# A new hand-written order, and two loads moved ahead of another, in a one-core kernel of chunked attention and a cosine feed-forward layer

## The chip, the core and the metric

One core of a Trainium2 chip runs the whole program. It has five engines with queues of their own: TensorE (PE in the profile, its weight loads PEld), VectorE (DVE), ScalarE (ACT), GpSimd (POOL) and SyncE (SP), which issues nearly all loads and stores. The metric is device time in microseconds (us) of one execution; less is better. Fast comparisons use the median of several runs.

## The reference

```python
scores = scale * np.matmul(q_c, k_c.transpose(0, 1, 2, 4, 3))   # chunks of 64 positions, 8 x 8 heads
scores = scores - np.max(scores, axis=-1, keepdims=True)
attn = np.exp(scores)
attn = attn / (np.sum(attn, axis=-1, keepdims=True) + 1e-09)
out = np.matmul(attn, v_c)
...
x = np.ascontiguousarray(attn_out.transpose(0, 2, 1, 3)).reshape(B * S, H * D)   # 4608 x 512
h = x @ w_in            # 512 x 2048
g = h * np.cos(h)
return (g @ w_out).astype(np.float32)    # 2048 x 512
```

Attention has batch 8, 8 heads, 576 positions and head size 64, and looks only within chunks of 64 positions. Its rows are the 4608 tokens of the layer behind it.

## The kernel before

The tokens are cut into tiles of 512. For each tile the kernel loads queries and keys (`qt`, `kt`) and values (`vt`) of four pairs of heads, 256 KB each, and makes for each pair: the scores on TensorE; their largest value, the difference, the exponential, its sum and the quotient on VectorE, ScalarE and GpSimd; the transposes of the result on TensorE (`transposed`, L656) with a copy to `pts`; and the products with the values (`acc<-pts,vt`). The weighted values are split into a high and a rest part (`weighted`, L736 and L739), which are the tile's `x`. Then come `h<-x,w_in` and, after h * cos(h), `acc<-w_out,g`. Each product of 32-bit numbers is made of three matmuls on such parts (`x_hi`, `x_lo`). w_in and w_out lie in 16 blocks each, which arrive as 64-bit numbers, 512 KB a block, and are made into 32-bit parts by ScalarE (`half`, L434, and `w`, L432), VectorE (L427) and GpSimd or VectorE. For the later tiles, products are made from sums and differences of blocks of 256 rows, seven products in place of eight; their sums go out to memory (`sums`, `diffs`, `combo`) and come back by loads (`block_pair`, `g_load`, `w_load`).

All of this is cut into 3646 pieces. `piece` appends each to the list `work`, with its engine, the pieces it waits for and, for some, another engine that may do it. Nothing of it runs in the order of that list. RANK is a table written out by hand into the program: it gives each piece its place in one order over all engines, and each engine gets its pieces in that order. ELSEWHERE lists the pieces that run on their other engine (a copy by VectorE instead of ScalarE, a TENSOR_TENSOR by GpSimd instead of VectorE, or the reverse). So each engine's queue is fixed, and an instruction whose input isn't there holds back everything behind it.

Ahead of the pieces stand loads: FIRST_LOADS is a list of 24, issued one after the other by SyncE at the start (`load`, L348). `('qk', 1, 0)` is queries and keys of the second tile's first pair of heads, `('in', 0)` the first block of w_in, `('v', 0, 0)` the first values. For the first tile `load_qk` gives the keys to ScalarE's queue (L481); for the others both to SyncE's. The buffers of `qt` and `kt` are four each, so that the second tile's first pair takes the place of the first tile's first pair.

For the attention of the first tile the work of one head pair runs through several engines, and the order decides which of the pieces of four pairs goes first. The numbers of pieces named below are places in `work`.

Of the kernel before, what the change touches and what calls it, by code (L numbers as in the profile page):

```python
# [71 lines left out]
    ('qk', 0, 0), ('qk', 0, 1), ('qk', 0, 2), ('qk', 0, 3), ('in', 1), ('qk', 1, 0),  # L72
    ('in', 0), ('v', 0, 0), ('v', 0, 1), ('in', 2), ('v', 0, 2), ('in', 4),
# [19 lines left out]
    27, 24, 33, 39, 42, 45, 15, 59, 68, 71, 54, 58, 64, 77, 81, 83, 69, 87, 96, 110, 90, 80, 115, 121, 125, 120, 92,  # L93
    134, 144, 148, 130, 139, 143, 146, 149, 155, 142, 167, 170, 173, 161, 172, 177, 182, 186, 176, 174, 180, 188,
    190, 189, 185, 194, 197, 201, 195, 192, 204, 212, 216, 213, 205, 222, 225, 227, 219, 221, 232, 238, 241, 233,
    229, 236, 247, 252, 244, 262, 264, 268, 273, 258, 270, 272, 277, 281, 279, 271, 291, 295, 298, 283, 284, 288,
    306, 322, 308, 299, 312, 314, 317, 327, 313, 331, 339, 341, 330, 316, 335, 345, 347, 346, 354, 357, 360, 369,
    356, 348, 362, 370, 373, 371, 377, 388, 391, 393, 382, 365, 387, 396, 397, 400, 390, 404, 407, 409, 403, 394,
    406, 416, 420, 424, 413, 442, 444, 448, 426, 435, 438, 441, 452, 453, 449, 459, 464, 468, 458, 440, 462, 466,
    472, 0, 13, 1, 3, 4, 5, 2, 7, 8, 12, 6, 9, 11, 17, 10, 22, 28, 31, 18, 26, 36, 14, 16, 20, 23, 30, 35, 41, 50,  # L100
    19, 21, 25, 37, 46, 40, 47, 29, 34, 38, 49, 56, 43, 53, 44, 51, 60, 63, 74, 65, 70, 57, 61, 67, 75, 79, 73, 76,
    32, 48, 55, 66, 78, 84, 86, 89, 88, 94, 98, 102, 93, 101, 105, 108, 72, 91, 137, 156, 95, 104, 99, 159, 168,
    171, 111, 114, 109, 112, 117, 200, 147, 150, 128, 131, 181, 231, 178, 223, 245, 251, 256, 255, 259, 52, 62, 82,
    85, 100, 107, 116, 119, 124, 127, 97, 103, 106, 113, 118, 123, 126, 129, 132, 136, 122, 135, 140, 145, 153, 158,
    162, 141, 151, 138, 133, 154, 152, 163, 165, 175, 179, 184, 169, 157, 166, 160, 164, 187, 191, 202, 209, 218,
    220, 183, 198, 196, 203, 193, 199, 207, 210, 214, 217, 234, 215, 224, 206, 208, 211, 226, 230, 235, 243, 246,
    250, 228, 254, 239, 237, 242, 240, 248, 253, 261, 266, 269, 267, 276, 274, 294, 249, 257, 275, 280, 282, 293,
    305, 307, 278, 263, 292, 260, 265, 286, 290, 296, 300, 303, 309, 301, 287, 289, 297, 285, 304, 527, 302, 525,
    321, 532, 318, 530, 548, 311, 315, 319, 324, 326, 328, 310, 333, 323, 332, 336, 334, 337, 340, 343, 349, 350,
    344, 320, 325, 329, 353, 352, 359, 363, 366, 368, 372, 367, 358, 338, 351, 342, 375, 378, 380, 383, 385, 386,  # L110
    384, 364, 355, 395, 361, 398, 401, 405, 408, 422, 427, 402, 376, 374, 381, 379, 411, 414, 417, 425, 428, 432,
    410, 429, 433, 419, 423, 445, 455, 457, 469, 474, 480, 489, 492, 497, 500, 508, 512, 544, 562, 528, 547, 554,
    555, 557, 565, 566, 571, 576, 574, 596, 575, 578, 586, 593, 597, 603, 613, 620, 636, 640, 421, 399, 392, 389,
    415, 431, 436, 439, 443, 446, 454, 437, 434, 467, 470, 430, 447, 450, 456, 465, 485, 487, 451, 476, 460, 473,
    479, 461, 471, 475, 483, 491, 495, 481, 463, 478, 499, 498, 490, 493, 496, 504, 507, 514, 486, 505, 494, 509,
    502, 510, 513, 515, 516, 521, 524, 511, 545, 503, 517, 559, 518, 526, 529, 541, 561, 564, 523, 543, 546, 534,
    520, 535, 538, 542, 551, 553, 558, 550, 536, 573, 556, 540, 567, 584, 587, 591, 594, 598, 560, 595, 583, 580,
    589, 570, 581, 590, 602, 604, 612, 601, 569, 592, 577, 585, 608, 610, 622, 625, 629, 633, 616, 628, 609, 607,
    611, 634, 638, 621, 623, 617, 631, 619, 626, 627, 630, 635, 637, 641, 642, 632, 656, 624, 643, 650, 645, 654,
    658, 668, 676, 677, 647, 671, 652, 646, 667, 661, 663, 666, 679, 689, 692, 675, 686, 662, 664, 659, 685, 695,  # L120
    699, 701, 705, 714, 700, 696, 690, 694, 717, 710, 712, 715, 718, 729, 735, 708, 734, 725, 731, 722, 720, 728,
    733, 740, 744, 747, 737, 418, 412, 533, 552, 599, 588, 660, 519, 477, 482, 484, 488, 539, 501, 506, 522, 531,
    579, 537, 549, 563, 568, 606, 572, 582, 600, 605, 615, 614, 618, 639, 644, 670, 648, 649, 674, 688, 697, 698,
    702, 653, 719, 750, 703, 713, 730, 758, 651, 657, 673, 680, 687, 721, 691, 742, 678, 732, 669, 684, 682, 711,
    672, 681, 655, 665, 723, 727, 716, 724, 736, 739, 726, 753, 766, 767, 772, 799, 801, 790, 793, 822, 824, 811,
    817, 830, 872, 885, 928, 910, 902, 916, 931, 943, 980, 992, 1007, 1031, 1008, 1020, 1075, 1049, 1072, 1079,
    1091, 1087, 1095, 1103, 1114, 1122, 1120, 1152, 1159, 1197, 1179, 1201, 1215, 1211, 749, 738, 842, 754, 765,
    757, 741, 826, 761, 783, 819, 776, 785, 880, 821, 889, 893, 816, 864, 895, 683, 693, 709, 746, 756, 763, 704,
    707, 745, 751, 774, 786, 780, 792, 796, 807, 868, 871, 878, 743, 748, 752, 755, 760, 771, 759, 762, 764, 769,
    778, 813, 805, 886, 891, 894, 904, 927, 938, 706, 777, 768, 770, 787, 775, 773, 779, 794, 782, 781, 784, 812,  # L130
    789, 788, 791, 804, 795, 798, 802, 806, 803, 810, 809, 815, 797, 800, 808, 827, 832, 836, 841, 844, 814, 820,
    825, 829, 818, 823, 828, 833, 835, 838, 862, 845, 847, 858, 851, 853, 940, 876, 896, 874, 861, 865, 921, 945,
    899, 905, 870, 883, 930, 988, 948, 890, 866, 898, 831, 834, 839, 857, 907, 909, 854, 877, 879, 884, 914, 929,
    936, 962, 964, 968, 971, 976, 979, 837, 840, 843, 846, 849, 860, 848, 852, 855, 863, 901, 961, 944, 983, 999,
    1003, 1013, 1033, 1038, 850, 856, 859, 873, 867, 869, 875, 903, 881, 882, 888, 900, 887, 892, 906, 908, 911,
    915, 913, 919, 923, 918, 922, 924, 926, 934, 897, 912, 917, 925, 952, 957, 969, 974, 920, 950, 954, 967, 932,
    935, 939, 946, 949, 953, 1036, 990, 986, 993, 981, 1024, 1040, 1048, 1055, 1074, 985, 989, 1000, 1078, 1025,
    996, 991, 1006, 1012, 1016, 1086, 1043, 933, 937, 941, 942, 951, 955, 958, 960, 959, 987, 956, 963, 977, 966,
    965, 970, 973, 998, 972, 975, 984, 995, 978, 982, 1022, 1002, 1005, 1026, 1009, 1014, 1017, 1011, 1021, 1019,
    1023, 1052, 994, 997, 1004, 1010, 1037, 1047, 1051, 1062, 1015, 1018, 1029, 1050, 1027, 1030, 1034, 1041, 1054,  # L140
    1068, 1076, 1112, 1090, 1110, 1085, 1089, 1099, 1153, 1127, 1146, 1092, 1101, 1148, 1115, 1133, 1131, 1100,
    1116, 1160, 1156, 1150, 1164, 1028, 1032, 1042, 1044, 1046, 1053, 1056, 1057, 1058, 1060, 1065, 1064, 1063,
    1067, 1071, 1073, 1070, 1080, 1083, 1082, 1081, 1094, 1118, 1097, 1102, 1161, 1105, 1108, 1163, 1107, 1111,
    1119, 1123, 1128, 1098, 1104, 1109, 1113, 1125, 1132, 1135, 1140, 1121, 1126, 1138, 1147, 1129, 1142, 1145,
    1151, 1117, 1130, 1136, 1154, 1143, 1139, 1155, 1158, 1220, 1172, 1225, 1249, 1261, 1169, 1245, 1252, 1157,
    1162, 1236, 1229, 1178, 1176, 1167, 1168, 1231, 1250, 1181, 1244, 1248, 1234, 1256, 1258, 1059, 1066, 1061,
    1084, 947, 1039, 1069, 1077, 1141, 1174, 1173, 1185, 1088, 1134, 1144, 1149, 1182, 1192, 1170, 1093, 1177, 1186,
    1001, 1045, 1096, 1137, 1180, 1184, 1124, 1165, 1190, 1195, 1175, 1189, 1106, 1199, 1035, 1191, 1166, 1171,
    1183, 1188, 1200, 1187, 1194, 1193, 1218, 1196, 1203, 1209, 1204, 1208, 1207, 1198, 1202, 1205, 1214, 1217,
    1223, 1228, 1232, 1206, 1210, 1221, 1226, 1213, 1219, 1224, 1242, 1237, 1246, 1312, 1297, 1309, 1295, 1240,  # L150
    1243, 1255, 1259, 1238, 1272, 1265, 1270, 1274, 1375, 1314, 1356, 1286, 1280, 1285, 1283, 1290, 1264, 1300,
    1308, 1212, 1216, 1230, 1233, 1247, 1257, 1227, 1235, 1239, 1254, 1262, 1263, 1267, 1271, 1275, 1327, 1330,
# [2430 lines left out]
```

## Time and profile before

| | us |
|---|---|
| median of three runs | 773.69 |
| the three runs | 773.27, 773.69, 774.88 |
| profiled execution | 774.28 |
| its span, from the first to the last instruction | 772.3 |
| TensorE busy in the span | 756.1 |
| VectorE busy | 678.9 |
| ScalarE busy | 529.7 |
| GpSimd busy | 343.0 |

The profiled execution stands 0.59 us above the median; 1.98 us of it lie outside the span. Busy time of an engine is the time in which any of its instructions runs. Matmuls overlap a little, and the ends given for them are modelled, so the times from start to start say more than their durations. A wait is put down to what came last. In brackets a timeline shows the idle time before an instruction and what ended it.

### The profile page before, as it was taken

What the parts mean: (1) busy time and instruction counts of PE and PEld (TensorE: products, weight loads), DVE (VectorE), ACT (ScalarE), POOL (GpSimd) and SP (SyncE); (2) the same over time, 40 slices, a digit from 0 to 9 for tenths busy, and PEclk for the clock granted to TensorE, in tenths of its full rate; (3) what the DMA queues carried; (4) which work ended last, traced back from release to release, by engine and by line L of the source; (5) the groups of instructions that cost most, each with busy time, mean ns of one, the idle gap of its engine ahead of it and who ended that gap; (6) DMA issues with size and microseconds to landing.
All of it is one profiled execution on the core that took longest, in us unless ns stands there. A gap on an engine that the chain in (4) does not pass through costs nothing. (4 is left out here: it accounts for less than half of the span.)

```text
span 772.3 us, 18060 instructions
## 1 busy us (share of the span) xinstructions
PE 756.1 (98%) x6680; PEld 684.6 (89%) x6680; DVE 678.9 (88%) x1138; ACT 529.7 (69%) x1064; POOL 343.0 (44%) x329
## 2 busy tenths in 40 slices
PE   7999999999999999999989999999999999999998
PEld 6788888888999888888889998888899989989997
DVE  5998889988999998989979989989999889878975
ACT  5998787465885556878876649879686556567532
POOL 1521224745589325745732235547601236454233
PEclk9999999999999999999999999999999999999999
DMA  9995023199989857898899956898899557999982
GB/s 347 409 418 217 1 94 115 53 328 339 375 306 317 290 176 266 285 324 267 301 337 348 351 196 224 273 327 314 295 378 337 190 184 253 310 315 328 360 288 90
DMA packets 127000, 210.92 MB, mean 273 GB/s; under 512 B 11712, under 2 KB 67008, under 8 KB 126912
## 3 DMA queue, kind: packets, MB, share of 16 engines
q1 hardware_dynamic: 126336, 208.71, 78.4%
q8 instruction: 53, 0.87, 0.4%
q10 hardware_dynamic: 576, 1.05, 0.4%
q14 instruction: 35, 0.29, 0.1%
HBM read 148.90 MB, written 60.82 MB: 272 GB/s over the span
## 5 line engine op out<-in xcount | busy, mean ns | idle before, releaser
L352 PE MATMUL h<-x,w_in 128*128 128x512 f32 (+1 forms) x960 | 225.4, 365 | 0.4 <-DVE w_in L373 0.2
L352 PEld LDWEIGHTS h<-x,w_in 128*128 128x128 f32 x960 | 168.8, 190 | 22.1 <-DVE g L777 0.7
L352 PE MATMUL acc<-w_out,g_hi 128*128 128x512 f32 (+1 forms) x720 | 172.5, 329 | 0.0
L352 PEld LDWEIGHTS acc<-w_out,g_hi 128*128 128x128 f32 x720 | 124.0, 190 | 12.5
L352 PE MATMUL acc<-w_out,g_lo 128*128 128x512 f32 (+1 forms) x360 | 117.4, 326 | 0.0
L352 PE MATMUL h<-w_in,w_in 128*128 128x512 f32 (+1 forms) x384 | 98.6, 355 | 1.3 <-ACT h L1018 1.1
L373 POOL TENSOR_TENSOR w_in<-w_in,w_in 128x512 f32<-128x512 f32 (+2 forms) x41 | 48.8, 1195 | 60.0 <-ACT w_in L1031 22.2
L352 PEld LDWEIGHTS h<-w_in,w_in 128*128 128x128 f32 x384 | 65.5, 190 | 10.7 <-ACT h L1018 2.9
L352 PEld LDWEIGHTS acc<-w_out,g_lo 128*128 128x128 f32 x360 | 68.6, 190 | 4.7
L369 ACT CAST g_hi<-w_in 128x512 fp32r<-128x512 f32 x71 | 44.0, 623 | 34.7 <-PE acc L352 16.2
L1031 ACT ACTIVATE w_in<-w_in 128x512 f32<-128x512 f32 x96 | 57.8, 628 | 12.1 <-DVE w_in L1027 11.8
L373 POOL TENSOR_TENSOR g_lo<-w_in,g_hi 128x512 fp32r<-128x512 f32 x32 | 42.0, 1314 | 36.6 <-ACT g_hi L369 18.5
L373 DVE TENSOR_TENSOR g_lo<-w_in,g_hi 128x512 fp32r<-128x512 f32 x62 | 45.5, 738 | 5.8 <-ACT g_hi L369 3.5
L369 ACT CAST g_hi<-x 128x512 fp32r<-128x512 f32 x52 | 32.2, 623 | 22.7 <-PE acc L352 12.0
L373 POOL TENSOR_TENSOR g_lo<-x,g_hi 128x512 fp32r<-128x512 f32 x9 | 12.3, 1376 | 75.7 <-ACT g_hi L369 75.7
L1024 ACT ACTIVATE w_in<-w_in 128x512 int32<-128x512 f32 x56 | 34.2, 627 | 16.2 <-DVE w_in L1021 11.9
L352 PE MATMUL a<-w_in,w_in 128*128 128x512 f32 (+1 forms) x204 | 43.1, 350 | 0.9 <-ACT w_in L369 0.6
L352 PE MATMUL a<-x,w_in 128*128 128x512 f32 (+1 forms) x192 | 41.2, 353 | 0.0
L352 PE MATMUL acc<-w_in,g_hi 128*128 128x256 f32 x240 | 41.0, 275 | 0.0
L1027 DVE SCALAR_TENSOR_TENSOR w_in<-w_in,w_in 128x512 f32<-128x512 int32 x56 | 37.8, 698 | 3.4 <-ACT w_in L1024 2.8
L373 DVE TENSOR_TENSOR g_lo<-x,g_hi 128x512 fp32r<-128x512 f32 x47 | 35.4, 766 | 5.3 <-ACT g_hi L369 5.1
L352 PE MATMUL acc<-x,g_hi 128*128 128x256 f32 x232 | 39.6, 275 | 0.0
(318 smaller groups left out, 1942.4 us busy)
## 6 DMA issues: line engine op xcount, KB each, us to landing
w_in<-combo SPq DMA_DIRECT2D x84, 512.0 KB, 5.4
w_in<-sums SPq DMA_DIRECT2D x64, 256.0 KB, 5.1
combo<-w_in SPq DMA_DIRECT2D x56, 256.0 KB, 4.3
w_in<-combo SPq DMA_DIRECT2D x56, 256.0 KB, 5.4
x<-sums SPq DMA_DIRECT2D x48, 256.0 KB, 5.0
qt<-in_qT_dram SPq DMA_DIRECT2D x36, 256.0 KB, 5.4
w_in<-in_w_in_dram SPq DMA_DIRECT2D x16, 512.0 KB, 9.5
kt<-in_kT_dram SPq DMA_DIRECT2D x32, 256.0 KB, 5.4
```

The source lines that it names most:

```text
L352: kept(nc.tensor.matmul(*args, **kw))
L369: kept(nc.scalar.copy(out=out, in_=in_))
L373: kept(eng.tensor_tensor(out, a, b, op=op))
L1024: kept(nc.scalar.activation(g.bitcast(I32), h, AF.Identity, bias=0.25, scale=0.5 / math.pi))
L1027: kept(nc.vector.scalar_tensor_tensor(g, g.bitcast(I32), -2.0 * math.pi, h, op0=ALU.mult, op1=ALU.add))
L1031: kept(nc.scalar.activation(g, g, AF.Sin, bias=0.5 * math.pi))
```

## The change

FIRST_LOADS has the second tile's first queries and keys behind the first block of w_in and the first values instead of ahead of them. The order table is new: of 3646 places 3342 differ, by a median of 4 places and at most 356. On TensorE 289 of 962 pieces keep their place and most of the others move by five places or less. ELSEWHERE has 363 entries in place of 373; 236 are in both. VectorE has 1096 pieces in place of 1084, GpSimd 264 in place of 275, ScalarE 836 in place of 837, TensorE and SyncE as many as before. The pieces themselves are the same.

```diff
 FIRST_LOADS = [
-    ('qk', 0, 0), ('qk', 0, 1), ('qk', 0, 2), ('qk', 0, 3), ('in', 1), ('qk', 1, 0),
-    ('in', 0), ('v', 0, 0), ('v', 0, 1), ('in', 2), ('v', 0, 2), ('in', 4),
+    ('qk', 0, 0), ('qk', 0, 1), ('qk', 0, 2), ('qk', 0, 3), ('in', 1), ('in', 0),
+    ('v', 0, 0), ('qk', 1, 0), ('v', 0, 1), ('in', 2), ('v', 0, 2), ('in', 4),
     ('v', 0, 3), ('in', 3), ('out', 0), ('qk', 1, 1), ('out', 1), ('qk', 1, 2),
     ('qk', 1, 3), ('out', 2), ('in', 5), ('v', 1, 0), ('v', 1, 1), ('out', 3),
 ]
...
 RANK = (
-    27, 24, 33, 39, 42, 45, 15, 59, 68, 71, 54, 58, 64, 77, 81, 83, 69, 87, 96, 110, 90, 80, 115, 121, 125, 120, 92,
-    134, 144, 148, 130, 139, 143, 146, 149, 155, 142, 167, 170, 173, 161, 172, 177, 182, 186, 176, 174, 180, 188,
...
+    26, 22, 33, 39, 42, 34, 16, 52, 65, 69, 57, 43, 61, 68, 77, 80, 73, 86, 99, 108, 94, 89, 115, 121, 124, 120,
+    102, 131, 146, 155, 130, 138, 145, 149, 151, 161, 143, 167, 169, 172, 166, 152, 174, 183, 185, 176, 171, 180,
...
 ELSEWHERE = (
-    4, 8, 9, 14, 19, 23, 28, 33, 34, 48, 49, 53, 58, 63, 79, 83, 89, 94, 98, 99, 103, 104, 108, 118, 123, 128, 129,
-    134, 138, 139, 144, 148, 154, 159, 184, 186, 188, 211, 238, 239, 244, 246, 271, 281, 288, 309, 331, 342, 343,
...
+    4, 8, 9, 13, 14, 19, 23, 24, 33, 34, 43, 53, 58, 59, 63, 68, 89, 93, 94, 99, 104, 108, 109, 114, 123, 124, 128,
+    129, 134, 138, 144, 148, 149, 153, 182, 186, 188, 238, 239, 241, 244, 246, 256, 280, 281, 288, 331, 354, 355,
...
```

What the two tables say at the places that the prediction speaks of, each as piece numbers in an engine's order:

| place | before | after |
|---|---|---|
| TensorE, first tile: transposes of pair 0 (189) and pair 1 (196), weighted values of pair 0 (191), second tile's first scores (217) | 189, 191, 196, 217 | 189, 196, 191, 217 |
| ScalarE, first tile: copy of the first transposes (190), lower half of the first w_in block (1) | 190, 1, 0 | 1, 190, 0 |
| first tile's quotients: pair 0 (182), pair 1 (184) | VectorE, GpSimd | GpSimd, VectorE |
| TensorE, block pieces between the products 1708 and 1710 | two (1538, 1616) | five (1537, 1604, 1619, 1605, 1606) |
| ScalarE, pieces from 1728 to the cast 1745 | 1728, 1724, 1824, 1754, 1726, 1730, 1732, 1733, 1740, 1745 | 1728, 1754, 1724, 1730, 1732, 1726, 1733, 1745 |
| pieces of 400 to 500 us that change their engine | | 12 from GpSimd and 12 from ScalarE to VectorE, 8 from VectorE to ScalarE, 5 to GpSimd |

## Rows read from the trace of the kernel before

**Rows 1.** The page, busy us, share of the span and instructions of each engine.

```profile
PE 756.1 (98%) x6680; PEld 684.6 (89%) x6680; DVE 678.9 (88%) x1138; ACT 529.7 (69%) x1064; POOL 343.0 (44%) x329
```

**Rows 2.** TensorE's waits: us in total, times, longest us.

```profile
PE acc L352 <- DMA vt<-in_v_dram: 2.8, 1, 2.8
PE a L352 <- ACT g_hi L369: 1.6, 1, 1.6
```

**Rows 3.** Timeline of TensorE, 11 to 35 us: start, us, instructions, idle before.

```profile
11.36 0.63 PE L656 MATMUL a<-ident,e 128*128 128x128 f32 x4 [0.41 <-DVE e L373]
14.74 1.14 PE L352 MATMUL acc<-pts,vt 64*64 64x64 f32 x32 [2.75 <-DMA vt<-in_v_dram]
15.80 1.11 PE L656 MATMUL a<-ident,e 128*128 128x128 f32 x4
16.85 1.59 PE L352 MATMUL a<-kt,qt 64*64 64x64 f32 x30
...
19.30 0.92 PE L352 MATMUL h<-x,w_in 128*128 128x512 f32 x3
...
34.19 2.86 PE L352 MATMUL h<-x,w_in 128*128 128x512 f32 x12
```

**Rows 4.** Windows: length, busy us of PE, PEld, DVE, ACT, POOL, clock, DMA share, GB/s.

```profile
20.00:40.00 20.00, 18.21 (x285) 15.02 (x285) 19.35 (x37) 18.70 (x35) 9.61 (x8) 1.00 1.03 410
400.00:500.00 100.00, 99.19 (x888) 93.27 (x888) 88.69 (x146) 70.00 (x143) 40.16 (x37) 0.98 0.83 285
```

**Rows 5.** Timeline of TensorE, the holes at 306, 384 and 399 us.

```profile
306.02 0.48 PE L352 MATMUL h<-w_in,w_in 128*128 128x512 f32 x1 [0.20 <-ACT h L1018]
...
384.64 1.56 PE L352 MATMUL a<-w_in,w_in 128*128 128x512 f32 x6 [0.63 <-ACT w_in L369]
...
398.94 0.49 PE L352 MATMUL a<-w_in,g_hi 128*128 128x256 f32 x2 [1.62 <-ACT g_hi L369]
```

**Rows 6.** Windows around the holes of rows 3 and 5, columns as in rows 4.

```profile
14.50:18.00 3.50, 3.26 (x58) 2.84 (x60) 1.89 (x5) 2.32 (x6) 1.00 (x1) 0.51 1.04 406
384.00:388.00 4.00, 3.37 (x17) 2.96 (x17) 3.96 (x6) 2.66 (x5) 1.81 (x2) 1.00 0.85 214
400.00:404.00 4.00, 4.00 (x23) 4.00 (x23) 3.30 (x7) 2.62 (x5) 1.11 (x1) 0.57 1.05 375
404.00:408.00 4.00, 4.00 (x38) 4.00 (x38) 2.65 (x6) 3.20 (x6) 0.00 (x0) 1.00 1.00 329
```

**Rows 7.** Timeline of SyncE's queue at the start, loads as they are issued.

```profile
4.62 0.33 SPq L349 DMA_DIRECT2D w_in<-in_w_in_dram  x1
5.87 0.33 SPq L349 DMA_DIRECT2D qt<-in_qT_dram  x1
...
6.72 0.43 SPq L349 DMA_DIRECT2D w_in<-in_w_in_dram  x1
```

**Rows 8.** Timeline of ScalarE, the split of the first w_in block.

```profile
14.03 0.66 ACT L434 ACTIVATE half<-w_in 128x512 uint32<-128x512 uint32 x1 [1.41 <-DMA w_in<-in_w_in_dram]
```

**Rows 9.** Timeline of ScalarE, 384 and 398 us.

```profile
384.00 0.58 ACT L369 COPY w_in<-a 128x512 f32<-128x512 f32 x1 [0.63 <-DVE w_in L686]
...
398.26 1.66 ACT L369 CAST g_hi<-x 128x512 fp32r<-128x512 f32 x3
```

**Rows 10.** Timelines of GpSimd and VectorE, 386 us.

```profile
386.30 1.59 POOL L373 TENSOR_TENSOR w_in<-w_in,w_in 128x512 f32<-128x512 f32 x1 [2.09 <-DMA sums<-w_in]
...
386.08 0.68 DVE L373 TENSOR_TENSOR w_in<-w_in,w_in 128x512 f32<-128x512 f32 x1
386.68 1.77 DVE L373 TENSOR_TENSOR pts<-w_in,e 128x512 f32<-128x512 f32 x1
```

**Rows 11.** The chain that ended last, around 571 us: start, us, what.

```profile
563.93 5.88 DMA x<-sums
...
571.32 2.72 PE a L352 x22
```

**Rows 12.** Timeline of VectorE, its wait for TensorE before that.

```profile
508.25 0.69 DVE L367 COPY e<-a 128x512 f32<-128x512 f32 x1 [1.72 <-PE a L352]
```

415 rows, old and new, of tables (ELSEWHERE, RANK) are left out of this document.

## The prediction

> **What bounds the kernel now.** I read the page's busy times first, then TensorE's waits, then windows and timelines around each wait, and last the chain that ended last. The page has TensorE busy for 756.1 us of a span of 772.3 [rows 1]: 16.2 us of idle time is all that any reordering can win back, apart from clock. The reader is to see that this is a TensorE-bound kernel with a few holes. The waits name the holes [rows 2]: 2.8 us for the first values (vt), 1.6 us in one wait for a g_hi cast. The rest is start, tail and waits that are shorter, each under 1.5 us.
>
> The timeline of the first 35 us [rows 3] shows the biggest hole: the transposes of the first head pair end at 11.99, and the first weighted values begin at 14.74, when vt lands. Until 34.19 there are further short waits. In 20 to 40 us VectorE is busy for 19.35 of 20 us and TensorE for 18.21 [rows 4], so there VectorE, not TensorE, sets the pace; this matters for what an earlier start is worth. Of the later holes three matter here, at 306.02, 384.64 and 398.94 [rows 5].
>
> The windows show a second cost [rows 6]. In 14.5 to 18.0 the granted clock is 0.51, just after the 2.75-us hole, and in 400 to 404 it is 0.57, just after the hole of 1.62 us: the lower of the two levels (1.2 instead of 2.4 GHz) for most of this window. In 404 to 408 it is 1.00, with 38 matmuls in 4 us, some 0.105 us each; the window before has 23. It lacks 15, or 1.6 us, of which I count 1.5. After the hole of 0.63 us at 384.64 the clock stays at 1.00.
>
> **Own time and median.** The profiled execution took 774.28 us, its span is 772.3, and 1.98 lies around it. It stands 0.59 above the median of 773.69. I make the sum against 774.28 and carry it to the median. 0.2%, about what a measurement can tell here from no change, is 1.5 us.
>
> **The loads.** In SyncE's queue the first queries and keys of the second tile (qt and kt, 512 KB together) stand ahead of the first block of w_in and the first values [rows 7]. qt is issued at 5.87 only, 1.25 us after the load before it: its buffer is the one that the first scores read. Moved behind both, it costs the two loads nothing, and they have 512 KB less ahead of them. At the 410 GB/s of 20 to 40 us [rows 4] this is 1.28 us. The w_in block was in use at 14.03 [rows 8] and would be at 12.75; vt was used at 14.74 [rows 3] and would land at 13.46. The bounds: no gain at all (14.74), and, if the queue's gap at 5.87 closes as well, another 1.25 us (12.2). I take 13.46, since the data rate, not the issue, is what a queue of 512-KB loads shows. The second tile's scores, which need the moved qt, begin at 16.85 [rows 3]; landing behind 768 KB, they still come before 15.
>
> **The order around them.** The new order puts the transposes of the second head pair before the first weighted values on TensorE, and on ScalarE the split of the w_in block (0.66 us [rows 8]) before the copy of the first transposed tile, which the weighted values read. So the copy starts at 12.75 + 0.6 = 13.35 at the earliest, and with some 0.55 the weighted values start at 13.9, 0.84 earlier than now. The second transposes (1.11 us at the lower clock [rows 3]) already lie in the hole before. The scores that start at 16.85 would then start at 13.9 plus 0.7 to 1.1, about 14.8: 2 us earlier. Splitting the 2.75-us hole in two also leaves nothing like it ahead of 14.5, and the 0.51 stretch [rows 6] may go; its cost is inside the 2 us.
>
> How much of the 2 us is left at 34.19, from where TensorE runs without a gap for over 100 us? VectorE was idle for 1.61 of 3.5 us in 14.5 to 18 [rows 6] and for 0.65 in 20 to 40 [rows 4]. Its own queue can move up by no more than such idle time, 2.26 us, and its order there is as dense as before. I take half: **-1.1 us** (bounds 0 and -2.2).
>
> **The stall at 384.64.** TensorE waits 0.63 us for ScalarE's copy, which waited 0.63 us for VectorE's transposes [rows 5, 9]. The new order puts five instead of two block pieces (three matmuls of 256 columns, 0.3 us by that 0.105) ahead of the waiting matmuls. Three more are 0.9 us, which covers 0.63: **-0.63** (bounds 0 and -0.63). The moved pieces are missing as cover elsewhere; this stands below.
>
> **The stall at 398.94.** It waits for the first of three g_hi casts, of which each takes 0.55 us of ScalarE [rows 9]. In the new order two fewer ScalarE pieces stand between the last chain it shares and this cast: 2 x 0.55 = **-1.1** of the 1.62 us (bounds 0 and -1.62). What is late next is the chain whose pieces now follow the cast. If the hole falls from 1.62 to some 0.5 us, it is as short as that of 384.64, and the drop after it goes: **-1.5** (bounds 0 and -1.5).
>
> **What the order gives back.** At 306.02 a filler of six matmuls of 512 columns (1.3 us, as the row at 384.64 has them with 1.56 to the modelled end) no longer stands ahead of the waiting matmuls, while on VectorE two scores pieces give way: 0 to +1.3, I take +0.7. Between 400 and 500 us the new table of other engines moves twelve pieces from GpSimd and twelve from ScalarE to VectorE, and thirteen back: eleven more there, at 0.69 us a piece [rows 10], 7.6 us. VectorE is idle for 11.3 of these 100 us and TensorE for 0.8 [rows 4], so the idle time hides them unless it lies in the wrong places: 0 to +7.6, I take +0.8. The other moves of pieces by a few places have stretches without a TensorE wait on both sides and are taken at nothing; if their cover is gone, they cost what the small waits cost now, under 1 us each.
>
> For the price of a piece moved to VectorE there is a row that bears on it. GpSimd's TENSOR_TENSOR runs from 386.30 to 387.89, and a VectorE TENSOR_TENSOR that starts inside it takes 1.77 us instead of 0.68 [rows 10]. By the Trainium skill, page "SBUF — State Buffer", section "Who interferes with whom", a VectorE instruction with two inputs in SBUF and a GpSimd instruction that reads SBUF exclude each other, and the later one waits for the whole of the first; the trace agrees with its 1.77 us. By that rule each of the seven net pieces that leave GpSimd (twelve out, five in) could free VectorE of up to 1.1 us, so that the 7.6 us would be balanced instead of hidden; the sum would then be 0.8 us better, 770.1.
>
> **The sum.** -1.1 -0.63 -1.1 -1.5 +0.7 +0.8 = -2.83. On the profiled execution 774.28 becomes 771.4; on the median it is 773.69 - 2.83 = **770.9 us**.
>
> After 571 us the chain that ended last is TensorE almost without a break, so what is won before should stay. But at 571.32 TensorE follows a chain of a load (x from sums, issued 563.93), a cast and a subtraction [rows 11]. A TensorE that comes 3 us early waits there, unless that chain moves too. Before it VectorE waited 1.72 us for TensorE at 508.25 [rows 12], so it does move in part; the give-back above leaves room for the rest.
>
> **The rivals.**
> A. *The forecast*, 0.49: faster, 770.9, its own range 769.2 to 772.1.
> B. *Everything comes*, 0.12: the start keeps 2.2, both stalls go whole (0.63 and 1.62), the clock gives 1.5, nothing comes back: -5.95, 767.7. For it: each hole has one named cause that the order touches. Against it: VectorE at 19.35 of 20 us.
> C. *The change does nothing to the end*, 0.23: the values land earlier, but VectorE holds the pace until 34 us, and the stall at 398.94 goes only to come back a few pieces later, with its drop of the clock: 0 to -1.4, about 773.2. For it: VectorE has 0.65 us of idle time in 20 to 40 [rows 4], and TensorE's wait at 571.32 hangs on a chain that holds no long TensorE work. Against it: TensorE has no other hole of over 1 us from 34 to 571.
> D. *Slower*, 0.16: VectorE becomes the bound in 400 to 500 us. The 7.6 us of added pieces land on the path there; the rest of the sum is -3.6, so it is 773.69 - 3.6 + 7.6 = 777.7 at the full price. It decides from 5.1 us on (slower by 0.2%), that is when two thirds of the pieces fall where TensorE waits. For it: VectorE has 88.69 of 100 us before the pieces come [rows 4]. Against it: 11.3 us idle.
>
> Faster by over 0.2% are A, almost whole, and B: 0.61. Within 0.2% is C and a sliver of A: 0.23. Slower is D: 0.16. The range runs from 767.7, B's full price, to 775.0, inside D; it leaves out half of B, where more than that price is won, and most of D.
>
> **What would show it.** vt's wait on TensorE at 13 to 14 us instead of 14.74, and no granted clock near 0.5 after it; h's first matmuls (19.30) near 17.5 to 18.5; TensorE's unbroken run from 34.19 starting about 1.1 us earlier. No wait at the place of 384.64, and under 1 us at that of 398.94 with a clock of 1.00 behind it. VectorE at about 95 of 100 us in the stretch that was 400 to 500. The prediction is wrong if the values don't land earlier, if a new TensorE wait of over 1 us appears anywhere between 34 and 571, above all one with a drop of the clock behind it, or if the wait at 571.32 grows by what was won before.

## The result and the profile after

The changed kernel is slower: 780.40 us (median of seven runs, 776.24 to 781.49) against 773.82 for the kernel before (seven runs, 773.27 to 774.96). The ratio is 1.0073 with a 95% interval of 1.0053 to 1.0092. The forecast was 770.9, in a range of 767.7 to 775.0. The profiled execution took 779.37 us, its span is 777.5 against 772.3.

The page of the changed kernel, busy time of each engine, answers to [rows 1]:

```profile
PE 757.2 (97%) x6680; PEld 684.9 (88%) x6680; DVE 685.0 (88%) x1148; ACT 528.0 (68%) x1063; POOL 334.0 (43%) x320
```

TensorE does the same work and idles for 20.3 us in place of 16.2. So some 4 us of the 5.2 by which the span grew are idle time. The other 1.1 are busy time. The mean granted clock of the two spans hardly differs (0.996 before, 0.995 after), so the lower clock in sum doesn't account for it; the drain that each wait adds (last section) may. TensorE's waits in the changed kernel (us in total, times, longest):

```profile
PE a L351 <- DMA kt<-in_kT_dram: 2.9, 2, 2.2
PE h L351 <- DVE w_in L372: 1.5, 2, 1.3
...
PE a L351 <- ACT w_in L368: 1.3, 3, 1.0
PE a L351 <- DVE g_lo L372: 1.3, 2, 0.9
PE a L351 <- POOL x L372: 1.2, 1, 1.2
PE acc L351 <- DVE g_lo L372: 1.0, 2, 0.8
```

The waits of [rows 2] are gone: neither vt nor a g_hi cast holds TensorE up. In their place stand a wait for keys and several waits of about 1 us. The start, TensorE's timeline of the changed kernel, to be held against [rows 3]:

```profile
13.03 0.66 PE L655 MATMUL a<-ident,e 128*128 128x128 f32 x4 [0.68 <-ACT pts L368]
13.68 0.69 PE L351 MATMUL acc<-pts,vt 64*64 64x64 f32 x32
15.13 1.05 PE L351 MATMUL a<-kt,qt 64*64 64x64 f32 x29 [0.75 <-DMA kt<-in_kT_dram]
...
17.09 0.46 PE L351 MATMUL h<-x,w_in 128*128 128x512 f32 x1
...
23.67 1.97 PE L351 MATMUL a<-kt,qt 64*64 64x64 f32 x32 [2.17 <-DMA kt<-in_kT_dram]
25.57 4.17 PE L351 MATMUL h<-x,w_in 128*128 128x512 f32 x9
...
37.22 2.86 PE L351 MATMUL h<-x,w_in 128*128 128x512 f32 x12
```

Up to 17.09 nearly all went as forecast: the first weighted values start at 13.68 (13.9 forecast, 14.74 before), the scores at 15.13 (14.8, 16.85), the first h at 17.09 (17.5 to 18.5, 19.30). The scores waited 0.75 us for the keys that the change moved back, a wait that I hadn't counted. Then TensorE stands for 2.17 us in front of scores of the second tile's second head pair, whose keys haven't landed, and the nine matmuls behind take 4.17 us in place of some 2.2. The matmuls that began at 34.19 begin at 37.22: the lead of 2.2 us has become a lag of 3.0. The wait alone only used up the lead: these scores start at 23.67, and before the change they started at 23.59. The lag arises behind it. Windows of the changed kernel (columns as in [rows 4]):

```profile
20.00:40.00 20.00, 16.66 (x250) 13.70 (x242) 14.96 (x30) 12.95 (x24) 7.21 (x6) 0.83 1.03 412
23.00:31.00 8.00, 7.33 (x85) 6.00 (x87) 3.47 (x8) 2.73 (x6) 2.38 (x3) 0.59 1.04 409
400.00:404.00 4.00, 3.67 (x31) 3.48 (x32) 4.00 (x9) 3.37 (x7) 0.00 (x0) 1.00 1.04 360
400.00:500.00 100.00, 98.03 (x885) 91.36 (x886) 92.44 (x158) 67.76 (x140) 33.13 (x30) 1.00 0.85 285
```

The granted clock is 0.59 in 23 to 31 us, right behind the wait for keys: for most of that window it is the lower of the two levels. From the start of the scores to the next matmuls it is 1.90 us there (23.67 to 25.57) in place of 1.05 before (23.59 to 24.64), and the nine matmuls behind take 4.10 to the next start in place of some 2.0. Together that is 2.9 us, nearly the whole lag. VectorE, which I took to set the pace in 20 to 40 us, is busy for 14.96 us there in place of 19.35; 4.7 us of its idle time are waits for TensorE's scores. So at 23.67 a load sets the pace (the DMA share of 1.03 stayed), and behind it TensorE at the lower clock does.

TensorE's later waits in the changed kernel; the first two rows answer to the second and third of [rows 5]:

```profile
386.82 1.56 PE L351 MATMUL a<-w_in,w_in 128*128 128x512 f32 x6 [0.19 <-ACT w_in L368]
...
399.87 0.49 PE L351 MATMUL a<-w_in,g_hi 128*128 128x256 f32 x2 [0.17 <-ACT w_in L368]
...
420.76 0.38 PE L351 MATMUL a<-w_in,g_lo 128*128 128x256 f32 x1 [0.94 <-DVE g_lo L372]
...
534.88 1.53 PE L351 MATMUL h<-x,w_in 128*128 128x512 f32 x6 [0.64 <-DMA w_in<-combo]
...
562.63 0.27 PE L351 MATMUL h<-w_in,qt 64*64 64x64 f32 x2 [1.29 <-DVE w_in L372]
...
753.02 0.71 PE L351 MATMUL a<-w_out,x 128*128 128x256 f32 x4 [1.20 <-POOL x L372]
```

In this trace the middle came as forecast: 0.63 became 0.19, 1.62 became 0.17, and the clock behind is 1.00. (Experiment 6 shows that the second of these isn't there in other traces of the same order.) But waits that I had taken at nothing stand at 421, 535, 563 and 753.

**Where the 5.17 us of the spans arose.** The new order and the old one have done the same set of pieces after 120, 1200 and 2100 of 3646, so the kernel can be cut there. Taking the starts of the same three matmuls in each trace (old: 34.19, 294.65, 467.93; new: 37.22, 298.08, 468.88) and the ends of the spans gives the four stages:

| stage of the order | before | after | difference |
|---|---|---|---|
| pieces to 120 | 34.19 | 37.22 | +3.03 |
| 120 to 1200 | 260.46 | 260.86 | +0.40 |
| 1200 to 2100 | 173.27 | 170.81 | -2.46 |
| from 2100 | 304.40 | 308.62 | +4.22 |

These are one execution of each kernel. How far one execution can mislead is seen in the experiments below: in eleven traces with the old loads and the old first stage, that of the kernel before among them, the mark of 34.19 lies between 33.28 and 36.00, in the middle at 34.90.

### The profile page after: what moved, and what is told of

It reads as the page before. It is cut to its first block, busy times and chain, and to the rows that moved or that the text cites. A ratio compares the mean times of both kernels' runs of the same rounds, so it can differ in the third digit from the quotient of the medians.

```text
span 777.5 us, 18058 instructions
## 1 busy us (share of the span) xinstructions
PE 757.2 (97%) x6680; PEld 684.9 (88%) x6680; DVE 685.0 (88%) x1148; ACT 528.0 (68%) x1063; POOL 334.0 (43%) x320
## 3 DMA queue, kind: packets, MB, share of 16 engines
q10 hardware_dynamic: 576, 1.05, 0.4%
## 4 chain that ended last, share of the span: by engine, by line
PE 77%; DMA 8%; DVE 8%; ACT 4%; issue 2%; SPq 1%; POOL 1%; ACTq 0%; DVEq 0%
PE acc L351 30%; PE h L351 29%; PE a L351 18%; DMA kt<-in_kT_dram 2%; DMA x<-diffs 2%; DVE w_in L372 1%; DVE w_in L1026 1%; DMA vt<-in_v_dram 1%; DMA x<-sums 1%; DMA sums<-w_in 1%; DMA w_in<-combo 1%; DMA out_dram<-w 1%; DVE g_lo L372 1%; ACT w_in L1023 1%; SPq L348 1%
## 5 line engine op out<-in xcount | busy, mean ns | idle before, releaser
L351 PE MATMUL h<-x,w_in 128*128 128x512 f32 (+1 forms) x960 | 227.9, 368 | 2.1 <-DVE x L738 0.7
L372 POOL TENSOR_TENSOR g_lo<-w_in,g_hi 128x512 fp32r<-128x512 f32 x34 | 46.2, 1360 | 88.8 <-ACT g_hi L368 72.5
L372 POOL TENSOR_TENSOR w_in<-w_in,w_in 128x512 f32<-128x512 f32 (+2 forms) x34 | 39.5, 1168 | 60.2 <-ACT w_in L1030 29.0
L368 ACT CAST g_hi<-w_in 128x512 fp32r<-128x512 f32 x74 | 45.9, 623 | 24.3 <-PE acc L351 9.2
L368 ACT CAST g_hi<-x 128x512 fp32r<-128x512 f32 x49 | 30.3, 622 | 27.4 <-PE acc L351 11.7
L1026 DVE SCALAR_TENSOR_TENSOR w_in<-w_in,w_in 128x512 f32<-128x512 int32 x56 | 40.0, 731 | 3.1 <-ACT w_in L1023 2.3
L372 DVE TENSOR_TENSOR g_lo<-x,g_hi 128x512 fp32r<-128x512 f32 x50 | 38.0, 770 | 2.6 <-ACT g_hi L368 2.0
L351 PEld LDWEIGHTS a<-w_in,w_in 128*128 128x128 f32 x204 | 33.2, 190 | 5.1 <-PE h L351 0.7
```

The source lines that it names most:

```text
L351: kept(nc.tensor.matmul(*args, **kw))
L368: kept(nc.scalar.copy(out=out, in_=in_))
L372: kept(eng.tensor_tensor(out, a, b, op=op))
L1026: kept(nc.vector.scalar_tensor_tensor(g, g.bitcast(I32), -2.0 * math.pi, h, op0=ALU.mult, op1=ALU.add))
```

## The experiments

The theory of the start, **late keys** (K): the new order asks for the second pair's keys earlier, while they can land no earlier, since the bytes ahead of them are the same. Its rivals: the moved loads themselves cost the time, or nothing of the start matters and the loss is VectorE's. For the rest the question was which stage loses by itself. The kernels keep both pairs of tables and go through them in stages; all have this function, and the diff of each is its list of stages:

```diff
+def in_stages(work, stages):
+    done = set()
+    for rank, elsewhere, upto in stages:
+        for i, by in in_order(work, rank, elsewhere)[:upto]:
+            if i not in done:
+                done.add(i)
+                yield i, by
...
-    for i, by in in_order(work, RANK, ELSEWHERE):
+    STAGES = [(RANK, ELSEWHERE, 1200), (NEW_RANK, NEW_ELSEWHERE, 2100), (RANK, ELSEWHERE, 3646)]
+    for i, by in in_stages(work, STAGES):
```

All were timed in five rounds against the kernel before on the same chip. Over these comparisons its own runs lay between 771.25 and 777.82, so ratios are more to be trusted than medians. Where an interval holds 1, no change is shown. "Stage" times are read from one trace each, between the marks of the table above.

**1. Only the loads.** Edit: the FIRST_LOADS of the change, both tables old.

> Only the two loads moved, both tables as before. Theory K (late keys: the new start lost because its order asks for the keys of the second tile's second pair when they cannot have landed, waits 2.17 us for them and then runs at the lower clock): the old order asks for them later, so no wait for keys, the values about 1.2 us earlier, and with VectorE setting the pace to 34 us the time is 772.5 to 774.0 beside 773.8. Rival M (the moved loads themselves cost the time, since the second tile's first keys land later): about 776.8, +3.

Measured: 772.89 us, ratio 0.9983 (0.9969 to 0.9996). The loads don't cost: M falls. In this kernel's trace TensorE is early too, and waits for the same keys:

```profile
13.16 0.69 PE L352 MATMUL acc<-pts,vt 64*64 64x64 f32 x32 [0.67 <-ACT pts L369]
...
23.13 1.05 PE L352 MATMUL a<-kt,qt 64*64 64x64 f32 x29 [1.54 <-DMA kt<-in_kT_dram]
```

So part of my expectation failed: the old order has this wait as well, 1.54 us, as soon as TensorE is early. It doesn't even take the moved loads: in experiment 9 loads and first stage are the old ones, no low clock held TensorE back in that trace, and it waits too:

```profile
23.06 1.17 PE L580 MATMUL a<-kt,qt 64*64 64x64 f32 x32 [1.76 <-DMA kt<-in_kT_dram]
```

In the five traces that wait at this place (the changed kernel and experiments 1, 2, 7 and 9) the scores start at 23.06 to 23.67, in either order and with either list of loads. That was the limit of the start in them. What lies behind it differs: here the granted clock is 1.00 in 23 to 31 us, and the matmuls of 34.19 begin at 33.35.

**2. The loads and the new first stage.** Edit: `STAGES = [(NEW_RANK, NEW_ELSEWHERE, 120), (RANK, ELSEWHERE, 3646)]`, new FIRST_LOADS.

> The loads moved and the first 120 pieces (to about 34 us) in the new order, the rest of the old order. K: the wait of about 2.2 us for keys near 23.7 us and the lower clock behind it are there, and the time is 776.5 to 777.5, +3.0. Rival S (the start is made up later; the loss is many small waits of the later stages, VectorE with more pieces): 773.3 to 774.5.

Measured: 775.55 us, 1.0025 (1.0007 to 1.0042). The new first 120 pieces turn a gain of 0.17% into a loss of 0.25%. S falls; the size, some 1.9 us, is smaller than the 3.0 of one trace. In this trace the wait for the keys is 1.37 us (less than in experiment 1), the granted clock behind it is 0.50 in 23.8 to 27.2, and the mark lies at 35.73. So in the traces it is the low clock behind the wait, more than the wait, that parts 1 and 2. Both traces of the new first stage with these loads have it (waits of 2.17 and 1.37 us); the three of the old first stage with waits of 1.54, 1.90 and 1.76 us (experiments 1, 7 and 9) have a clock of 1.00. Why the one order gets it and the other doesn't is not shown.

**3. The same with the keys one place earlier.** Edit to 2:

```diff
-    ('v', 0, 3), ('in', 3), ('out', 0), ('qk', 1, 1), ('out', 1), ('qk', 1, 2),
+    ('v', 0, 3), ('in', 3), ('qk', 1, 1), ('out', 0), ('out', 1), ('qk', 1, 2),
```

> The kernel of the new first 120 pieces, with the second tile's second queries and keys one place earlier in the list of loads, ahead of the first block of w_out: 512 KB less ahead of them, 1.25 us. Theory K (late keys): TensorE's wait for them, 1.37 us there, falls to 0.1 to 0.3, the drop of the clock behind it goes where it came, and the time is 772.8 to 774.3, at least 1.3 us under the 775.55 of the same order without this. Rival V (the new start is slow because of VectorE's and ScalarE's order, and the wait only shows where the slack is): the wait shrinks but another takes its place before 35 us, and the time stays within 0.7 us of 775.5.

Measured: 772.91 us, 0.9996 (0.9984 to 1.0008). One swap of loads takes back 0.29%, the whole loss of the new start against the kernel before; V falls. TensorE's timeline of this kernel:

```profile
21.85 1.15 PE L580 MATMUL a<-kt,qt 64*64 64x64 f32 x32 [0.53 <-DMA kt<-in_kT_dram]
25.57 1.15 PE L580 MATMUL a<-kt,qt 64*64 64x64 f32 x32 [0.43 <-DMA kt<-in_kT_dram]
```

The one wait is now several short ones for keys, 1.19 us in all (0.53, 0.43 and 0.23) against 1.37 in experiment 2; but the clock of 20 to 40 us is 1.00 in place of 0.91, and the mark lies at 33.55 in place of 35.73. The intervals of 2 and 3 only just touch. So for the new order K holds: the place of these keys in the list of loads decides its loss, and in the traces most of that loss is the clock behind the one long wait.

**4. The old order with the keys earlier.** Edit: the FIRST_LOADS of 3, both tables old.

> Both tables old; of the loads the change's two moves, and the second queries and keys of the second tile also one place earlier. The old order with the moved loads alone took 772.9, with a wait of 1.54 us for these keys. K: the wait falls to about 0.3 and 1.0 to 1.3 us of it are won: 771.5 to 772. Rival P (VectorE sets the pace to 34 us, as the prediction had it): 772.5 to 773.3.

Measured: 773.85 us, 1.0009 (0.9997 to 1.0022). No gain; against experiment 1 (0.9983, up to 0.9996) by the ratios the swap costs some 0.26%. Here the wait moved on to the third pair's keys (1.11 us at 26.20), and a new one of 0.32 us stands at 42.48 for GpSimd's part of w_out, whose first block is now loaded later. K's forecast for this order failed. A likely reason, not tested, is that no low clock followed the wait here, so there was little to win by mending it.

**5. The new stage of 34 to 294 us alone.** Edit: `[(RANK, ELSEWHERE, 120), (NEW_RANK, NEW_ELSEWHERE, 1200), (RANK, ELSEWHERE, 3646)]`, loads old.

> Only pieces 120 to 1200 of the order (about 34 to 294 us) new, loads and the rest old. The changed kernel's trace shows two waits of TensorE there that the old one hasn't, 0.78 us for a g_lo at 166 and 0.35 us for a g at 170, less a wait of 0.12 at 160: if the stage stands alone, 774.5 to 775.2, +1.0. If they come from arriving 3 us late at their loads (rival), 773.2 to 774.2.

Measured: 775.15 us, 1.0025 (1.0010 to 1.0041). The stage takes 261.36 us in this trace; in the sixteen traces with the old pieces there it takes 260.04 to 260.76. The waits of the changed kernel are there without its lag of 3 us, so the stage makes them itself:

```profile
163.41 0.48 PE L580 MATMUL acc<-w_out,g_lo 128*128 128x512 f32 x1 [0.78 <-DVE g_lo L601]
167.26 2.86 PE L580 MATMUL h<-x,w_in 128*128 128x512 f32 x12 [0.34 <-DVE g L1005]
```

**6. The new stage of 294 to 468 us alone.** Edit: the list shown above, loads old.

> Only pieces 1200 to 2100 of the order (about 294 to 468 us) in the new order, loads and all else old. K, with the middle stage right as forecast (holes of 0.63 and 1.62 us small, no drop of the clock near 400): the new trace gained 3.9 us there and lost 0.9 at 420 and some at 455, so 770.0 to 771.5. Rival D of the prediction (the eleven pieces more on VectorE between 400 and 500 us cost): 775 to 777.

Measured: 773.34 us, 0.9990 (0.9974 to 1.0006). Neither: D falls, but the gain is nearer 1 us than 3, and by the times of this run alone it isn't told from none. The stage takes 170.96 us in this trace, and 170.4 to 170.9 in the three others with the new pieces. In the twelve traces that have the old pieces there and no drop of the clock near 400 it takes 171.1 to 172.6. The drop that I had priced at 1.5 us is in two of fourteen traces with the old pieces only, that of the kernel before (173.27) and that of experiment 2 (174.10).

The wait that was to go from 1.62 to some 0.5 us didn't go, other than in the trace of the changed kernel. The same matmul in experiments 6, 7 and 8, which all have the new pieces here:

```profile
397.63 0.49 PE L580 MATMUL a<-w_in,g_hi 128*128 128x256 f32 x2 [0.88 <-ACT w_in L597]
```

```profile
395.95 0.49 PE L580 MATMUL a<-w_in,g_hi 128*128 128x256 f32 x2 [0.95 <-ACT w_in L597]
```

```profile
396.28 0.49 PE L580 MATMUL a<-w_in,g_hi 128*128 128x256 f32 x2 [1.07 <-ACT w_in L597]
```

In the fourteen traces with the old pieces it is 0.22 to 1.68 us, in the middle 1.2. The wait of 384.64 did go: 0.63 to 0.76 us in all fourteen, at most 0.36 in the four.

**7. This stage with the loads.** Edit: the same list, with the FIRST_LOADS of the change.

> The change's two moves of loads, and the new order only for pieces 1200 to 2100 (about 294 to 468 us); the rest of the order old. The loads alone gave -0.17%, this stage alone -0.1%, and its profile was 1.2 to 2.3 us shorter in the stage. If the parts add up: 771.4 to 772.2, a ratio near 0.9975. If a shorter stage is given back after 468, as the profile of that stage alone showed (306.2 us after it in place of 304.3 to 305.0): 772.4 to 773.2.

Measured: 771.21 us, 0.9973 (0.9958 to 0.9989). The two good parts add up, and this kernel is faster than the one before; that it is faster than either part alone is likely, but the intervals overlap. **8.** The stage joined to experiment 3 (`[(NEW, 120), (old, 1200), (NEW, 2100), (old, 3646)]`, in short):

> The new first 120 pieces with the second queries and keys loaded one place earlier, and the new pieces 1200 to 2100; the rest of the order old. The first gave 0.9996, the second 0.9990. If they add up: 772.2 to 773.0. If the middle is given back after 468: 773.2 to 774.

Measured: 772.04 us, 0.9985 (0.9965 to 1.0004), as the sum of its parts has it, but not told from no change. In this trace, with the first stage and the loads of experiment 3, the clock of 20 to 40 us is 0.92: the swap of loads doesn't always keep it at 1.00.

**9. The new stage from 468 us on alone.** Edit: `[(RANK, ELSEWHERE, 2100), (NEW_RANK, NEW_ELSEWHERE, 3646)]`, loads old.

> Only pieces from 2100 on (from about 468 us) in the new order. The trace of the changed kernel lost 4.2 us after 468, in waits of 0.64, 1.29, 0.96 and 1.20 us: if these belong to the order there, 777 to 778.5. If they come from the kernel arriving late, at another place against its loads (rival), 773.3 to 775.

Measured: 777.15 us, 1.0036 (1.0020 to 1.0053). The stage loses by itself, and most of all; 308.13 us in the trace. Its two longest waits there:

```profile
532.65 1.53 PE L580 MATMUL h<-x,w_in 128*128 128x512 f32 x6 [1.33 <-DMA w_in<-combo]
...
749.27 0.71 PE L580 MATMUL a<-w_out,x 128*128 128x256 f32 x4 [0.91 <-POOL x L601]
```

SyncE's queue in the same trace shows the first wait's load, issued at 525.98 right behind two stores. The load ahead of these stores was issued by 523.31; the first store left at 524.99, when VectorE's sum (`half`, the last line, from VectorE's timeline) had just ended:

```profile
522.88 0.43 SPq L577 DMA_DIRECT2D kt<-in_kT_dram  x1
524.99 0.38 SPq L2215 DMA_DIRECT2D sums<-half  x1
525.41 0.47 SPq L2215 DMA_DIRECT2D sums<-g  x1
525.98 1.17 SPq L577 DMA_DIRECT2D w_in<-combo  x2
...
524.51 0.41 DVE L601 TENSOR_TENSOR half<-w_in,w_in 128x256 f32<-128x256 f32 x1
```

**10. Both repaired.** Edit to 9:

```diff
+    ahead = {2431: 2408} if rank is NEW_RANK else {}
-    place = sorted(range(len(work)), key=lambda i: (rank[i], i)) if rank
+    place = sorted(range(len(work)), key=lambda i: (rank[ahead.get(i, i)] - (i in ahead) / 2, i)) if rank
...
+    BACK = (3552, 3562, 3574)
-    (NEW_RANK, NEW_ELSEWHERE, 3646)
+    (NEW_RANK, [i for i in NEW_ELSEWHERE if i not in BACK], 3646)
```

> The kernel with the new order from piece 2100 on, with two repairs in it: on SyncE the load 2431 goes ahead of the store 2408, which waits for GpSimd and VectorE, and the pieces 3552, 3562 and 3574 go back from GpSimd to VectorE. Theory Q (the late stage loses by its queues: a load held up behind a store, and GpSimd late with a product's input): the waits of 1.33 us near 532 and of 0.91 near 749 go, and of the 2.8 to 3.5 us that this stage lost about 2.2 come back: 774.3 to 775.3. Rival R (both are the place where a TensorE that came early had to wait anyway): new waits take their place and the time stays at 776.5 to 777.5.

Measured: 777.58 us, 1.0055 (1.0042 to 1.0067). Nothing won (five runs); Q falls. The wait near 532 is gone and that near 750 is 0.21, but a new one stands ahead of both:

```profile
517.28 1.56 PE L581 MATMUL h<-w_in,w_in 128*128 128x512 f32 x6 [1.10 <-DVE w_in L1250]
...
750.29 0.71 PE L581 MATMUL a<-w_out,x 128*128 128x256 f32 x4 [0.21 <-DVE x L602]
```

**11 and 12. The new order on the old engines, and the old order on the new engines, from 468 us.** Edits: in 9's list `(NEW_RANK, ELSEWHERE, 3646)`, and `(RANK, NEW_ELSEWHERE, 3646)`.

> From piece 2100 on the new order, but every piece on its old engine. New order and engines together there gave 776.5 to 777.2. Theory O (the order lost: TensorE's pieces stand where their inputs come late, and engines matter little): 776 to 777.5. Theory E (the engines lost: pieces moved between GpSimd and VectorE are done later or hold each other up): 773.5 to 774.7.

> From piece 2100 on the old order, but the new choice of engines. The counterpart of the one before. Theory O: 773.3 to 775. Theory E: 776 to 778. If both lose by themselves, order and engines fit only each other, and each misfit is worse than the whole: over 777 in both.

Measured: 784.19 us, 1.0142 (1.0122 to 1.0163), and 781.10 us, 1.0095 (1.0079 to 1.0111), of four and five runs. Both theories fall: each new table with the other's old partner is worse than the new pair is. Order and engines fit only each other, which says nothing yet of why the new pair loses to the old one.

**13 and 14. The late stage cut in two**, at piece 2800: `[(old, 2100), (NEW, 2800), (old, 3646)]`, and `[(old, 2800), (NEW, 3646)]`, in short.

> The new order and engines only for pieces 2100 to 2800 (about 468 to 594 us), all else old. The stage from 468 on lost 3.2 to 4.2 us in the profiles; its waits of 1.33 for a load near 532, and 0.54, 0.41, 0.19 and 0.27 near 560 and 587 in place of 0.90, lie here, and each wait costs some 0.17 more than its idle time, since the modelled end of a matmul lies that far behind the next start: about +2.2, so 775 to 776.5. If the late part is what loses: 773 to 774.3.

> The counterpart: new order and engines from piece 2800 on (about 594 us). The wait of 0.91 to 1.20 us for GpSimd's piece 3562 near 750 lies here: +1.1 to +1.4, so 774.3 to 775.2. If it only shows slack of a kernel that is early, 773 to 774.

Measured: 781.00 us, 1.0075 (1.0048 to 1.0102), and 774.90 us, 1.0021 (1.0003 to 1.0039). 13 is worse than the whole stage: at its joint TensorE waits 1.95 us for a g_lo at 603.86, with a granted clock of 0.51 in 604.7 to 608.1. Neither is in the trace of 9, so they are the joint's own, and the number doesn't measure the part. For at 2800 the two orders haven't done the same set of pieces: eight differ. 14 loses some 1.6 us by its times, but its trace doesn't show where: from 594 us on it has only two waits of over 0.15 us, 0.25 and 0.35, which the kernel before has too. The wait near 750 that was to lie here is 0.10 us.

**15 and 16. One repair in each part**: 14 with the three pieces back on VectorE, 13 with the load ahead of the store.

> As the one before, with the pieces 3552, 3562 and 3574 back on VectorE. Theory G (GpSimd's late piece is the loss of the last part): the wait near 750 falls from about 1.0 to 0.2, the stage is 0.9 to 1.1 us shorter, and the time within 0.5 us of the kernel before. Otherwise another wait takes its place and the time stays over 774.3.

> As the kernel with the new order for 468 to 594 us, with the load 2431 ahead of the store 2408 on SyncE. Theory H (the load held up behind a store that waits for other engines is the loss of that part): the wait near 532 goes, and 1.3 to 1.5 us of this part's loss with it: 774 to 775. Otherwise a wait near 517 for VectorE, as the kernel with both repairs had, takes its place, and nothing is won.

Measured: 774.61 us, 1.0007 (0.9991 to 1.0024), and 778.15 us, 1.0054 (1.0036 to 1.0073). Both lie lower than their counterparts, within the intervals. So the time of 15 is near what G forecast, but it isn't told from that of 14, and the traces speak against both theories. TensorE in 15, and then in 16:

```profile
749.25 0.71 PE L580 MATMUL a<-w_out,x 128*128 128x256 f32 x4 [1.01 <-DVE x L601]
```

```profile
518.18 1.56 PE L581 MATMUL h<-w_in,w_in 128*128 128x512 f32 x6 [1.54 <-DVE w_in L1250]
```

In 15 VectorE makes the input near 750, and TensorE waits 1.01 us for it; in 14 GpSimd makes it, and TensorE waits 0.10. In 16, with the load ahead, the wait is 1.54 us at 518. A wait that is mended comes back at another place, and the same order has a wait in one trace and not in another. So the waits that the profile names here aren't shown to be the causes of the loss. Nor is the engine that a wait is put down to always where it began: ahead of 753.02 in the changed kernel GpSimd had itself waited, for ScalarE.

```profile
749.96 1.34 POOL L372 TENSOR_TENSOR w_in<-g,w_in 128x512 fp32r<-128x512 f32 x1 [4.33 <-ACT w_in L368]
751.27 1.71 POOL L372 TENSOR_TENSOR x<-w_in,x 128x512 fp32r<-128x512 f32 x1
```

## Why the prediction was wrong

By stages the parts add up: +0.25% (loads and first stage), +0.25, -0.10 and +0.36 make +0.76%, against the measured +0.73%. Two steps of the prediction failed: it took VectorE, and not the next load, for the limit of the earlier start, and it took the moves of all other pieces at nothing.

**The loads** (right). The first w_in block is in use at 11.80 in the changed kernel, against 12.75 worked out and 14.03 before [rows 8]:

```profile
11.80 0.67 ACT L433 ACTIVATE half<-w_in 128x512 uint32<-128x512 uint32 x1
```

The gap in SyncE's queue at 5.87, which I had kept for the bound, no longer stands ahead of it; whether that made the rest isn't shown, for with the old loads the same block is in use at 12.71 in experiment 9. vt doesn't hold anything up in this trace. The loads alone make the kernel faster by 0.17%. Much of that may be the clock, which I had counted as "inside the 2 us": in ten of the eleven traces with the old loads and the old first stage the granted clock falls behind the wait for vt, and the mark lies at 34.16 to 36.00; where it stays at 1.00, it lies at 33.28 with the old loads (experiment 9) and at 33.35 and 33.51 with the moved ones (1 and 7).

**How much of the lead is left at 34.19: -1.1** (failed; it was +3.0 in the trace, and +0.25% with the loads' gain in it). I asked whether VectorE could follow, and not whether the next load could. With a DMA share of 1.03 in [rows 4] the loads of that stretch run back to back, and a TensorE that runs ahead meets the next one that is due, here the second pair's keys. In the trace of before it arrived at those scores only at 23.59, after its hole and the low clock of 14.5 to 18 [rows 6], when the keys were there; in experiment 9, with the same loads and first stage but no low clock, it came early and waited until 23.06. So this wait took the whole lead of 2.2 us. What made a lag of it, the granted clock of 0.59 behind the wait, the prediction had no term for. Experiments 1, 2 and 3 show it. With the old order the term would have been about right: the mark lies at 33.35 in experiment 1, 0.84 us earlier.

**The stalls at 384.64 and 398.94: -0.63 and -1.1** (the first right, the second by luck). In the changed kernel's trace they are 0.44 and 1.45 us less. The first is gone in all four traces with the new pieces. The second is 0.88 to 1.07 us in the three others: I had taken a wait of one execution, 1.62 us, that is 0.22 to 1.68 in the old order. In the new one the same matmul no longer waits for the cast but for another piece of ScalarE (`w_in`), the chain "whose pieces now follow the cast". Over the whole stage the four traces are some 1.3 us shorter than the middle of the twelve without a drop.

**The clock behind it: -1.5** (mechanism right, size wrong). The changed kernel has no drop there; but the old one has it in two traces of fourteen, those with the longest holes for this cast, 1.62 and 1.68 us. In experiment 9's trace a hole of 1.23 us for the same cast wasn't followed by a drop. I priced a chance event of one execution as a part of the kernel; by two in fourteen its worth is an estimated 0.2 us.

**What the order gives back: +1.5** (failed on the late stage). The wait at 306.02 didn't grow: the changed kernel has none there. The eleven pieces more on VectorE between 400 and 500 us didn't hurt: VectorE's 88.69 us became 92.44, half of the 7.6 reckoned. Over the whole stage from 294.65 it has 12 instructions more and is busy 156.20 us in place of 154.72, in the windows between the stage's marks. By the Trainium skill's page "SBUF — State Buffer", section "Who interferes with whom", a VectorE instruction with two SBUF inputs contends with a GpSimd instruction that reads SBUF, so a piece that leaves GpSimd can give VectorE back time that it had stood waiting. The trace agrees: of VectorE's TENSOR_TENSOR instructions with 512 columns in that stage, 8 of 122 took over 0.9 us before and 4 of 131 after, and their mean went from 744 to 712 ns. That other moved pieces are shorter may be a part of it too. But that the other moves of pieces by a few places "are taken at nothing" was the step that failed: between 34 and 294 us they cost 0.25%, from 468 on 0.36%. The fallback beside it, "under 1 us each", was too small as well: the waits at 562.63 and 753.02 are 1.29 and 1.20 us, and the first is the new wait of over 1 us between 34 and 571 that the prediction had named as a sign of being wrong. VectorE is busy for 90% of the time from 34 to 294 us and for 87% from 468 on, and I had followed four places out of hundreds.

**The rivals.** C and D didn't happen by their mechanisms: VectorE didn't hold the start back, and it didn't become the bound in 400 to 500 us. D had the direction, by luck. The result is slower for reasons that no rival had.

**What stays open.** Why the new order from 468 us on is 3 to 4 us longer. It is neither the order nor the engines alone; the single waits move when they are mended. This is the largest of the losses. Taking the start of one more matmul (608.05 before, 611.39 after), 2.4 us of it lie ahead of it and 1.8 behind. No single cause was found. Open too is why the clock falls behind the wait for keys in the new order and not in the old.

## What to carry to other kernels

Where loads run back to back, work moved forward gains only up to the next load that is due: look up when each of the next few inputs was issued and how many bytes stand ahead of it, before asking which engine is the bound; and look at the clock behind the wait, which cost more here than the wait. A wait of 1 or 2 us, or a drop of the clock, is to be checked in more than one trace before it is priced: the wait of 1.62 us that two terms of the prediction rest on was 0.22 to 1.68 in fourteen traces of the same pieces. And a hand-written order of thousands of pieces, and the choice of engines that goes with it, are one thing: half of it was worse than either whole, while whole stages, cut where both orders have done the same pieces, could be taken one by one, and the best two of them made a kernel that is 0.27% faster than the one before.

## What the runs showed of the hardware

By these traces a wait of TensorE costs a little more than the idle time that the profile shows for it. From the stage's mark at 468 us to the end experiment 9 took 3.7 us more than the kernel before, of which 2.6 were idle time; TensorE's busy time there rose from 298.24 to 299.40 us, for the same matmuls. The modelled end of a 512-column matmul lies 0.38 us behind its start, and the next one in an unbroken run starts after 0.215, so some 0.17 us of each wait are counted as busy. Experiment 9 has five waits of over 0.15 us more there than the kernel before; by this estimate they make some 0.8 of the 1.2 us, and the rest isn't explained.

The start of one order varies from run to run: with the old first stage and the old loads the matmuls of 34.19 began at 33.28 in experiment 9, where the granted clock is 1.00, at 34.19 in the kernel before, where it is 0.76 in 14 to 21 us, at 35.28 in experiment 6, where it is 0.51 there, and at 36.00 in experiment 13, with 0.51 as well. The landing of vt, with the same list of loads, varies too: the first weighted values start at 13.43 in experiment 9 and at 15.88 in experiment 13.
